# A routed expert kernel: conditional tiles moved in front of the last four static ones, and a skipped fallback path rewritten as a loop

## The chip, the cores and the metric

One core of a Trainium2 chip. The metric is device time in microseconds (us) of one execution. A profile is one execution, and its span (first to last instruction) is some 1.7 us shorter than the time of the same execution. Ratios and their intervals use only executions that the records call fast, on the same chip; the medians of the experiments are of all executions, slow ones included.

## The reference

Two stages in fp32. The first is chunked attention (4 batches, 8 heads, 768 tokens, heads of 64). The second is a mixture of 8 experts: each token goes to one expert, by an argmax over its logits or by inheriting the expert of the token in front of it.

```python
for s in range(S):
    fresh_e = int(np.argmax(logits[b, s]))
    e = fresh_e if s == 0 or local_gate[b, s] < 0.5 else prev_e
    prev_e = e
    p = softmax(logits[b, s])
    h = np.maximum(x[b, s] @ w1[e], 0.0)          # 512 -> 1024
    out[b, s] = p[e] * (h @ w2[e])                # 1024 -> 512
```

## The kernel before

Attention makes x, a router finds the expert of each token, and GpSimd scatters the rows to a DRAM buffer sorted by expert. The experts then work on tiles of 128 rows of one expert: gather the rows (GpSimd), turn (transpose) them on TensorE (`g_ps`, copied to SBUF by VectorE), first product (`h_ps`, relu by ScalarE), second product (`y_ps`, scaled by ScalarE), scatter to the output (GpSimd). 3072 tokens fill at least 24 tiles, which are static code. Up to 7 more are needed when experts' counts don't divide by 128; those are conditional on a count known only at run time, and with this input three of them run. The place behind them where all engines go on with unconditional code is called the join.

```python
for i in range(SURE):                            # SURE = 24
    ...                                          # (cut: gathers and weight loads ahead)
    w1_sb, w2_sb = tile_w[i]
    ht = hidden(xt, w1_sb, between.get(i, {}))   # 64 matmul instructions, relu
    ...
    if i + 1 < SURE:                             # the next tile's rows, turned ahead
        ahead = rows_turned(tiles, at_i, tile_xs[i + 1])
    stored = product(ht, w2_sb, tile_xs[i], past)   # 16 matmul instructions, scale, scatter
    xt, past = ahead

n_tiles = nc.values_load(n_i, ...)
for i in range(SURE - EARLY, NTILE - EARLY):     # the conditional tiles, at the end
    ctx.enter_context(tc.If(n_tiles > i))
    here = rest[:, i + EARLY - SURE]
    w1_sb, w2_sb = weights(late, i, pools[(i + EARLY) % 3])
    xt, past = rows_turned(late, i, here)        # turned when its turn comes
    product(hidden(xt, w1_sb), w2_sb, here, past)
```

The fast path takes exponentials without subtracting the maximum. It counts sums that stay in range, and if one doesn't, a general path computes everything again. Before, that path was the same function, unrolled a second time. With this input it is skipped; the branch that jumps over it is called the kept branch, after the count that it tests.

```python
everything(tc, *args, kept_i)
kept = nc.values_load(kept_i, ...)
with tc.If(kept < NT * H):
    everything(tc, *args, None)                  # the whole kernel once more, with shifted scores
```

## Time and profile before

| | before |
|---|---|
| time, median of 3 runs | 529.16 us |
| profiled span | 527.6 us |
| TensorE busy | 503.5 us (95%) |
| tile 0's first h starts at | 112.08 us |
| TensorE's last matmul ends at | 509.56 us |
| from there to the end | 18.02 us |

The last two rows come from the timeline of TensorE: the start of the last group, 502.52, plus its length, 7.03, with the nanoseconds that the view rounds off. Everything that argues about the end of the program below uses this one figure: span minus end of the last matmul. The profile calls TensorE PE, VectorE DVE, ScalarE ACT, GpSimd POOL and SyncE SP. In the page, the digits in 40 slices are busy tenths. In a view by source line, each row is operation, count, shortest/median/longest in ns, first and last start in us; a "q" behind an engine marks an instruction of its sequencer alone, which no busy figure counts.

### The profile page before, as it was taken

How to read it: one execution, taken by the hardware profiler on the slowest of the kernel's cores; microseconds unless marked ns; L12 is line 12 of the kernel's file. 1: busy time of each engine (PE TensorE's matmuls, PEld its weight loads, DVE VectorE, ACT ScalarE, POOL GpSimd, SP SyncE). 2: the span in 40 equal slices, each digit the busy share in tenths (PEclk: the TensorE clock that was granted, in tenths of full speed). 3: DMA queues.
4: the chain of work that ended last, by engine and by line, in shares of the span. 5: the costliest groups of instructions: out<-in, count | busy, mean ns of one | idle time of the engine just before them, and what ended most of it. 6: DMA issues, size and time to landing. Idle time of an engine off the chain costs nothing. (4 is left out here: it accounts for less than half of the span.)

```text
span 527.6 us, 9418 instructions
## 1 busy us (share of the span) xinstructions
PE 503.5 (95%) x3602; PEld 384.3 (73%) x3602; DVE 97.2 (18%) x361; ACT 113.0 (21%) x234; POOL 97.6 (19%) x142
## 2 busy tenths in 40 slices
PE   8999999999999999999999999999999999999960
PEld 5998989887677777777777777777777777777630
DVE  1456767653330000000000000000000000000000
ACT  3556555521101111111110111110110110111000
POOL 3000233444332111111001111122211011000000
PEclk9999999999999999999999999999999999999995
DMA  9987796799999999999889888899999899860000
GB/s 300 369 251 231 228 331 207 217 399 382 409 344 410 409 409 410 408 353 350 321 314 332 330 320 325 312 325 339 343 359 349 327 338 335 303 237 22 22 7 3
DMA packets 52761, 158.00 MB, mean 299 GB/s; under 512 B 7707, under 2 KB 11805, under 8 KB 52704
## 3 DMA queue, kind: packets, MB, share of 16 engines
q1 hardware_dynamic: 44352, 135.40, 71.0%
q0 software_dynamic: 6720, 20.78, 10.3%
q10 hardware_dynamic: 1632, 1.08, 0.7%
q8 instruction: 33, 0.54, 0.4%
q14 instruction: 24, 0.20, 0.1%
HBM read 144.62 MB, written 13.40 MB: 300 GB/s over the span
## 5 line engine op out<-in xcount | busy, mean ns | idle before, releaser
L647 PEld LDWEIGHTS h_ps<-gxt,w_sb 128*128 128x128 f32 x1664 | 189.6, 192 | 13.6 <-issue 10.5
L647 PE MATMUL h_ps<-gxt,w_sb 128*128 128x128 f32 x1664 | 190.6, 275 | 2.4 <-DVE gxt L583 1.6
L658 PE MATMUL y_ps<-w_sb,ht 128*128 128x512 f32 x416 | 182.8, 592 | 0.0
L658 PEld LDWEIGHTS y_ps<-w_sb,ht 128*128 128x128 f32 x416 | 77.0, 190 | 87.0 <-issue 85.9
L583 DVE COPY gxt<-g_ps 128x512 f32<-128x512 f32 x27 | 18.7, 692 | 315.9 <-PE g_ps L581 315.7
L650 ACT ACTIVATE ht<-h_ps 128x512 f32<-128x512 f32 x54 | 32.2, 597 | 156.4 <-PE h_ps L647 155.0
L663 POOL DMA_INDIRECT out_dram<-y,to x27 | 27.3, 1011 | 201.1 <-ACT y L662 166.6
L662 ACT ACTIVATE y<-y_ps,xs 128x512 f32<-128x512 f32 x24 | 16.5, 687 | 162.1 <-PE y_ps L658 155.9
L519 PE MATMUL o_ps<-vt,pt 128*96 128x65 f32 x512 | 49.3, 249 | 0.3 <-PE l_ps L519 0.2
L519 PEld LDWEIGHTS o_ps<-vt,pt 128*96 128x96 f32 x512 | 46.1, 165 | 2.7 <-issue 0.6
L364 POOL DMA_INDIRECT x_dram<-x,row x32 | 30.8, 961 | 75.3 <-DVE pick L309 65.5
L519 PEld LDWEIGHTS s_ps<-qt,kt 64*128 64x128 f32 x512 | 29.9, 188 | 6.1 <-issue 2.7
L519 PE MATMUL s_ps<-qt,kt 64*128 64x96 f32 x512 | 32.7, 277 | 0.4 <-ACT pt L211 0.4
L211 ACT ACTIVATE pt<-s_ps,mask_mid 128x256 f32<-128x256 f32 x72 | 28.1, 482 | 6.8 <-PE s_ps L519 6.6
L221 DVE TENSOR_TENSOR x<-o_ps,rinvs 96x256 f32<-96x256 f32 x64 | 26.3, 418 | 1.5 <-DVE rinvs L220 0.3
L262 ACT COPY xt<-xt_ps 128x384 f32<-128x384 f32 x32 | 15.3, 479 | 33.9 <-PE xt_ps L519 33.9
L660 POOL TENSOR_TENSOR to<-xs,past_late 128x1 int32<-128x1 int32 x19 | 3.5, 185 | 98.6 <-DMA out_dram<-y,to 94.1
L475 POOL DMA_INDIRECT xs<-x_dram,rows_late x19 | 18.4, 966 | 12.5 <-DMA x_dram<-x,row 7.0
L220 DVE RECIPROCAL rinvs<-o_ps 96x4 f32<-96x4 f32 x64 | 10.5, 171 | 35.7 <-PE o_ps L519 34.0
L519 PE MATMUL xt_ps<-ident,x 96*128 96x96 f32 x128 | 16.0, 247 | 0.0
L581 PE MATMUL g_ps<-ident,xs 128*128 128x128 f32 x88 | 13.3, 274 | 0.0
L519 PEld LDWEIGHTS xt_ps<-ident,x 96*128 96x128 f32 x128 | 12.7, 148 | 0.0
(160 smaller groups left out, 178.8 us busy)
## 6 DMA issues: line engine op xcount, KB each, us to landing
w_sb<-in_w_dram SPq DMA_DIRECT2D x216, 512.0 KB, 7.4
kt<-in_k_dram SPq DMA_DIRECT2D x32, 256.0 KB, 4.3
vt<-in_v_dram SPq DMA_DIRECT2D x28, 260.0 KB, 4.5
qt<-in_q_dram SPq DMA_DIRECT2D x32, 192.0 KB, 4.2
vt<-in_v_dram ACTq DMA_DIRECT2D x4, 260.0 KB, 4.8
x_dram<-x,row POOLq DMA_INDIRECT x32, 7.0
out_dram<-y,to POOLq DMA_INDIRECT x27, 7.6
xs<-x_dram,rows_late POOLq DMA_INDIRECT x19, 7.0
```

The source lines that it names most:

```text
L211: nc.scalar.activation(pt[:, :, :, c], st[:, :, :, c], ACT.Exp, bias=m[:, g:g + 1], scale=SCALE)
L221: nc.vector.tensor_tensor(x[:, 0:D].rearrange("p (a u d) -> p u a d", u=2, d=DH)[:, u], o_ps[:, :, 0:DH], rinv.to_broadcast([QB, HP, DH]), ...
L262: nc.scalar.copy(xt, xt_ps)
L364: ins = nc.gpsimd.indirect_dma_start(out=x_dram[:, :], out_offset=bass.IndirectOffsetOnAxis(ap=row[:, n:n + 1], axis=0), in_=x[0:QB, n].bi ...
L475: ins = nc.gpsimd.indirect_dma_start(out=xs.bitcast(I32), out_offset=None, in_=x_dram[:, :], in_offset=bass.IndirectOffsetOnAxis(ap=rows[: ...
L519: return f if shifted else lambda *a, **k: tc.keep_in_program_order(f(*a, **k))
L583: nc.vector.tensor_copy(xt, g_ps)
L647: nc.tensor.matmul(h_ps[:, m], lhsT=w1_sb[:, kk, P * (g + m):P * (g + m) + P], rhs=xt[:, kk], start=(kk == 0), stop=(kk == DK - 1))
L650: nc.scalar.activation(ht[:, g:g + 4], h_ps, ACT.Relu)
L658: nc.tensor.matmul(y_ps, lhsT=ht[:, m], rhs=w2_sb[:, m], start=(m == 0), stop=(m == FK - 1))
L662: nc.scalar.activation(y, y_ps, ACT.Copy, scale=xs[:, D:D + 1])
L663: return nc.gpsimd.indirect_dma_start(out=out, out_offset=bass.IndirectOffsetOnAxis(ap=to, axis=0), in_=y, in_offset=None, bounds_check=NT ...
```

## The change

Four things. The conditional tiles stand in front of static tile 20, so that the program ends in static code, and each turns the next one's rows ahead. The general path is a compact one: attention in order, then a loop over experts whose results are masked, with plain DMAs only. Tile 0's rows are turned before the last transposes of x. The ranks are transposed one block earlier. The rest (shared constants, where the count of sums is taken, buffers) makes room for it.

```diff
+BRANCH = SURE - 4
 with tc.If(kept < NT * H):
-    everything(tc, *args, None)
+    general(tc, q, k, v, w_gate, w_local, w1, w2, out, ident, back)
```
```diff
+def general(...):
+    ...                                    # (cut: attention, logits, prob[token, expert] masked by the choice)
+    with tc.For_i(0, E, 1) as e:
+        one_e = bass.ds(e, 1)
+        for kk in range(DK):
+            nc.sync.dma_start(w1_sb[:, kk], w1[one_e, kk].rearrange("o p f -> p (o f)"))
+        ...
+        for n in range(NB):
+            ...                            # hidden and product of 96 rows, as above
+            nc.vector.scalar_tensor_tensor(y[:, n], y_ps, mine[:, n], y[:, n], ALU.mult, ALU.add)
+    nc.sync.dma_start(out.rearrange("(n p) d -> p n d", p=QB), y)
```
```diff
+def maybe_tiles(ctx, xts):
+    n_tiles = nc.values_load(n_i, ...)
+    for j in range(NTILE - SURE):
+        i = SURE - EARLY + j
+        ctx.enter_context(tc.If(n_tiles > i))
+        w1_sb, w2_sb = weights(late, i, wa)
+        ht = hidden(xts[j % 2], w1_sb)
+        if j + 1 < NTILE - SURE:
+            rows_turned(late, i + 1, rest[:, j + 1], xt=xts[(j + 1) % 2])
+        product(ht, w2_sb, rest[:, j], late[2][:, i:i + 1])
 for i in range(SURE):
+    if i == BRANCH:
+        maybe_tiles(held_xt[1:])
...
+    if i + 1 == BRANCH:
+        rows_turned(late, SURE - EARLY, rest[:, 0], xt=held_xt[1])
-(the conditional tiles behind the loop)
```
```diff
-            plan_at(after, n + 5, rows, b)
+            plan_at(after, n + 4, rows, b)
...
-    plan_at(after, NB - 1, first_turned)          # behind the transposes of x
+        if n == NB - 1:
+            first_turned()                        # in front of them
```

## The prediction

> **What bounds the kernel now.** I read the page first: TensorE is busy nearly everywhere, so the time is TensorE's own work plus its gaps plus what lies before and behind it.
>
> ```profile
> PE 503.5 (95%) x3602; PEld 384.3 (73%) x3602; DVE 97.2 (18%) x361; ACT 113.0 (21%) x234; POOL 97.6 (19%) x142
> PE   8999999999999999999999999999999999999960
> DMA  9987796799999999999889888899999899860000
> ```
>
> The reader is to see a wall of nines on PE, a last slice of 13.2 us with none of it, and DMA that falls silent four slices earlier. The chain of waits is no help here: it holds one scatter and 0.2% of the span. So I went to the timeline of PE around the place where the static tiles end and the conditional ones begin (start, length, group, and in brackets the idle time before it and its releaser).
>
> ```profile
> 441.57 0.60 PE L581 MATMUL g_ps<-ident,xs 128*128 128x128 f32 x4
> 442.01 7.03 PE L658 MATMUL y_ps<-w_sb,ht 128*128 128x512 f32 x16
> 448.88 7.31 PE L647 MATMUL h_ps<-gxt,w_sb 128*128 128x128 f32 x64
> 456.02 7.03 PE L658 MATMUL y_ps<-w_sb,ht 128*128 128x512 f32 x16
> 462.89 0.60 PE L581 MATMUL g_ps<-ident,x 128*128 128x128 f32 x4
> 464.28 7.41 PE L647 MATMUL h_ps<-gxt,w_sb 128*128 128x128 f32 x64 [0.78 <-DVE gxt L583]
> 471.52 7.03 PE L658 MATMUL y_ps<-w_sb,ht 128*128 128x512 f32 x16
> ```
>
> A static tile is h (64 matmuls), g (four transposes of the next tile's rows) and y (16 matmuls). From the starts in the same view: h to g 7.14 us, g to y 0.44, y to the next h 6.87, so 14.45 us a tile. The last static tile has no g and takes 14.01. A conditional tile turns its own rows first, and then waits 0.78 us for VectorE's copy: h starts at 464.28 and the next at 479.78, so 15.50 us. With this input three of the seven conditional tiles run (27 scatters of results, 24 static), the last ending on PE at 509.56. The span ends at 527.6: 18.0 us follow PE's last matmul. What is in them the views by source line show, of the branch over the general path (L89) and of the end of the program (L751); columns are operation, count, shortest/median/longest ns, first and last start.
>
> ```profile
> L89 PEldq COMPARE_BRANCH  x1: 3387/3387/3387, 510.4 to 510.4; - x1
> L89 POOLq COMPARE_BRANCH  x1: 55/55/55, 513.9 to 513.9; - x1
> L89 POOLq EVENT_SEMAPHORE  x6: 17/30/43, 516.7 to 517.1; - x6
> L89 POOLq INC_SWDGE_SEM  x1: 1981/1981/1981, 517.2 to 517.2; - x1
> ...
> L751 POOLq DRAIN  x3: 40/107/7509, 519.2 to 527.3; - x3
> ```
>
> This is GpSimd's chain. The last result is issued at 511.1, then come a first INC_SWDGE_SEM at the join of the conditional tiles (2.03 us from 511.3, in the view of the helper's line), the branch at 513.9, its next instruction only at 516.7, a second INC_SWDGE_SEM of 1.98 us, and a DRAIN of 7.51 us from 519.2, after which 0.9 us of barrier end the program. All of it is on the path.
>
> **What the Trainium skill says.** "Runtime: NRT & Kernel Launch", section "Instruction fetch mechanics": a taken branch whose target is not in the two blocks at hand waits for a fetch. The trace agrees: branches within the tiles take PE 65 to 86 ns, the jump over the general path 3.39 us, and GpSimd resumes 2.7 us after its own. "DMA: Bandwidth & Descriptors", section "Anatomy of one DMA — SWDGE (gpsimd) path", puts one transfer at about 2.0 us plus its bytes over 436 GB/s. A full tile's 128 rows of 2 KB would then need about 2.6 us when nothing else moves (an estimate from that page). The page of this trace has a median of 7.6 us beside weight loads but 2.4 us for the last scatter, which is alone. No page tells how long the drain at the end is.
>
> **The change, part by part.**
>
> 1. *Conditional tiles in front of the last four static ones, with the rows turned ahead.* Inside a conditional tile the next rows are now turned before y, as in a static one. Before, from h of static tile 20 (405.53) to the end at 509.56, seven tiles took 104.03 us. As six tiles of 14.45 and a last one without g they take 6 x 14.45 + 14.01 = 100.71: 3.3 us less. Against it stand three costs. The third conditional tile also turns the rows of a fourth that doesn't run: 0.44 us in excess. In static tile 19 two sets of rows are turned back to back through a single PSUM buffer (g_ps): if nothing fills the gap, the second waits for VectorE's copy of the first, about the 0.78 us above; y is ready soon and may be put in front, so I take 0.4. And the join behind the conditional tiles stands in PE's way now. The trace shows what a join does: each engine waits for its own semaphore. PE passed it 0.05 us after its last matmul, with a branch of 0.2 us behind it; ScalarE passed it only after the last y, 0.83 us after that matmul. The first h of static tile 20 needs a PSUM buffer that ScalarE frees, counted beyond ScalarE's join, so I expect h to start about 1.0 us after the last y matmul instead of overlapping it by 0.16: 1.1 us. The long branch fetch (3.46 us on PE from 503.4) lies under the 16 y matmuls already queued and is free in both. Net: -3.3 + 0.4 + 0.4 + 1.1 = -1.4 us.
>
> 2. *Weights around the branch.* Tile 20's weights sit in the third buffer and are loaded ahead. Those of tile 21 can start only when PE is past its join. A tile's 4.2 MB at the 400 GB/s that the page shows in its best slices are 10.5 us, the first halves about 6 to 7; PE has 14.45 us of tile 20 meanwhile. The conditional tiles share two buffers instead of three, with a tile between release and use. Hidden: 0.
>
> 3. *End of the program.* The last tile is static, so the join, with its 2.03 us INC_SWDGE_SEM, is no longer behind the last scatter, but in the middle, where GpSimd has 14 us to spare. That takes about 2.0 us off the chain. The general path is now a loop without GpSimd's own DMAs, so GpSimd's jump over it may hit code at hand: up to 2.7 us more, of which waiting for the last full scatter to land (2.6 us) eats part; I take 1.0. The 7.51 us DRAIN I leave. Net -3.0.
>
> 4. *Tile 0's rows turned ahead.* At 110.0 to 112.1 PE does r_ps, g, waits, h:
>
> ```profile
> 109.58 0.50 PE L519 MATMUL xt_ps<-ident,x 96*128 96x96 f32 x4
> 110.01 0.54 PE L519 MATMUL r_ps<-ident,rank 8*96 8x8 f32 x8
> 110.64 0.66 PE L519 MATMUL g_ps<-ident,xs 128*128 128x128 f32 x4
> 112.08 2.05 PE L519 MATMUL h_ps<-gxt,w_sb 128*128 128x128 f32 x16 [0.78 <-DVE gxt L583]
> ```
>
> With g ahead of the xt transposes, their 0.43 us lie over the copy; the ranks' transposes move one block earlier, where VectorE finishes their input just then (its multiplications ran until 107.76, PE came by at 107.4), so a little is given back. Net -0.4.
>
> 5. *Kept count in tile 0 instead of tile 4, zero row from the warm-up tile, constants shared, general path rewritten.* Same matmuls, or off the path: PE's warm-up starts at 1.5 us and the first scores at 8.0, long after the masks are ready. The general path does not run with this input (all sums are in range). 0.
>
> Sum: -1.4 - 3.0 - 0.4 = -4.8, so 529.16 - 4.8 is about 524.4 us.
>
> **The rivals.** *A stall behind the join:* the weights of tile 21 come late, or PE must fetch instructions after the join, 3.4 us by the branch above. For it: nothing can be issued across the join, and all engines pass it in the same few microseconds. Against it: slack of several microseconds in the weights, and a fetch that the queue of y matmuls hid before. With it the gain of part 1 is lost and the time is near 528; a late load of some 7 us would make it 532. *The end stays as it is:* if the drain absorbs what is taken out in front of it (it waits for something that started with the last scatter, 15.6 us before it ends), only parts 1 and 4 remain: 527.4. *The end shrinks much more:* if the drain's 7.5 us are work left by the INC_SWDGE_SEM, and the skip path has none of it any more, the end falls from 18 us to some 6 to 8, and the time to 514 to 518. For it: the DRAIN follows the second INC directly, and the new general path uses no GpSimd DMA. Against it: two other GpSimd drains in the final barrier are short, which says only that something was pending. *TensorE's work itself* can't change: same matmuls, same clock.
>
> **Range and chances.** Parts 1 and 4 are worked out from repeated durations and may be off by 1.5 us together; the end is the wide part, from 0 to 5 us of gain as likely values. The range is 520.5 to 527.5. Faster by over 2% (below 518.8) needs the shrunken drain: 0.06. Slower by over 2% (over 539.7) needs a stall of 10 us, which I see nowhere: 0.02. Within 2%: 0.92.
>
> **What would show it.** Right: h of a conditional tile following y without the 0.78 us wait; one gap of about 1.1 us on PE at the first tile behind the join, released by ScalarE; two sets of g in tile 19; no INC_SWDGE_SEM between the last scatter and the kept branch; the same DRAIN of about 7.5 us; 15 us from PE's last matmul to the end. Wrong: weights as releaser of h or y, a gap of 3 us or more at the join, a longer or missing drain, or slower matmuls.

## More of the kernel before

One chip, on which e1 to e4, their repeats, e10 and e11 ran, granted TensorE 94 to 96% of its clock even in the fast executions, and the kernel before took 565 us there instead of 529. (Seven of the nine runs of the kernel before that e10, e11 and the repeats are compared with are from an earlier call on that chip.)

## The result, and the profile after

520.85 us (median of 4 fast runs, 520.23 to 521.97) against 529.15 of the kernel before. The ratio is 0.9839, with a 95% interval from 0.9815 to 0.9864. That is 8.3 us less: inside the range, at its lower end, and within 2%. The prediction had 4.8.

The page after: TensorE's busy time is the same within 0.1 us, its matmuls are four more (the rows of a conditional tile that doesn't run), the empty last slice has gone, and DMA shows a hole near the end and then two full slices. SyncE asks for the weights of static tile 21 only at 449.6 us, released by TensorE at the join.

```profile
PE 503.4 (97%) x3606; PEld 384.5 (74%) x3606; DVE 98.0 (19%) x362; ACT 113.2 (22%) x234; POOL 96.8 (19%) x141
PE   8999999999999999999999999999999999999991
DMA  9987797599999999999898899999998881299200
```

Where the 8.7 us of the span went, by marks that both timelines have:

| stretch | before | after | change | predicted |
|---|---|---|---|---|
| start to tile 0's first h | 112.08 | 111.95 | -0.13 | -0.4 |
| to the end of the last matmul | 397.47 | 396.05 | -1.43 | -1.4 |
| to the end of the program | 18.02 | 10.88 | -7.14 | -3.0 |

**The tiles.** The timeline of TensorE in the changed kernel around static tile 19 (start, length, group; idle time and releaser in brackets):

```profile
398.09 0.60 PE L677 MATMUL g_ps<-ident,xs 128*128 128x128 f32 x4
398.53 1.02 PE L754 MATMUL y_ps<-w_sb,ht 128*128 128x512 f32 x2
399.48 0.66 PE L677 MATMUL g_ps<-ident,x 128*128 128x128 f32 x4
399.97 6.17 PE L754 MATMUL y_ps<-w_sb,ht 128*128 128x512 f32 x14
405.98 0.60 PE L677 MATMUL g_ps<-ident,x 128*128 128x128 f32 x4
```

Two sets of rows are turned in tile 19, and two matmuls of y stand between them while VectorE copies the first: no wait. The third g belongs to the first conditional tile, which turns the rows of the second at once. Around the join:

```profile
434.88 0.60 PE L677 MATMUL g_ps<-ident,x 128*128 128x128 f32 x4
435.32 7.31 PE L743 MATMUL h_ps<-held_xt,w_sb 128*128 128x128 f32 x64
442.47 7.03 PE L754 MATMUL y_ps<-w_sb,ht 128*128 128x512 f32 x16
450.37 7.41 PE L743 MATMUL h_ps<-held_xt,w_sb 128*128 128x128 f32 x64 [0.87 <-ACTq _compat.py:109]
```

The waits of 0.78 us in front of each conditional h are gone. One gap of 0.87 us is left behind the join, and its releaser is ScalarE's sequencer at its own join. The instruction INC_SWDGE_SEM of GpSimd's queue, which stood behind the last scatter, is at the join here too:

```profile
_compat.py:109 POOLq INC_SWDGE_SEM  x1: 1939/1939/1939, 451.2 to 451.2; - x1
```

**The end.** GpSimd's part in the views of the branch over the general path, and of the end of the program:

```profile
L92 POOLq COMPARE_BRANCH  x1: 55/55/55, 509.7 to 509.7; - x1
```
```profile
L856 POOLq DRAIN  x3: 40/113/7862, 510.2 to 518.6; - x3
```

Before, 5.3 us lay between this branch and the drain (513.9 to 519.2), with a late start (GpSimd's next instruction came only at 516.7) and a second INC_SWDGE_SEM. Now it is 0.5 us, and there is no INC_SWDGE_SEM behind the last scatter at all. The drain itself is 7.86 us long, against 7.51.

**The start.** The last three microseconds in front of tile 0:

```profile
107.41 0.50 PE L613 MATMUL xt_ps<-ident,x 96*128 96x96 f32 x4
107.83 0.64 PE L613 MATMUL r_ps<-ident,rank 8*96 8x8 f32 x8
108.47 0.64 PE L613 MATMUL l_ps<-ident,lt_sb 128*96 128x128 f32 x4
108.95 1.50 PE L613 MATMUL o_ps<-vt,pt 128*96 128x65 f32 x16
110.28 0.61 PE L613 MATMUL g_ps<-ident,xs 128*128 128x128 f32 x4
110.73 0.49 PE L613 MATMUL xt_ps<-ident,x 96*128 96x96 f32 x4
111.95 2.05 PE L613 MATMUL h_ps<-held_xt,w_sb 128*128 128x128 f32 x16 [0.73 <-DVE held_xt L680]
```

g is ahead of xt as planned, and yet h still waits 0.73 us for VectorE's copy: g ends at 110.89, but VectorE is at work on x until about 111.3 and copies g only from 111.23 to 111.90. Whether the start gained anything is taken up under e5.

### The profile page after: what moved, and what is told of

It reads as the page before. It is cut to its first block, busy times and chain, and to the rows that moved or that the text cites. A ratio compares the mean times of both kernels' runs of the same rounds, so it can differ in the third digit from the quotient of the medians.

```text
span 518.9 us, 9415 instructions
## 1 busy us (share of the span) xinstructions
PE 503.4 (97%) x3606; PEld 384.5 (74%) x3606; DVE 98.0 (19%) x362; ACT 113.2 (22%) x234; POOL 96.8 (19%) x141
## 5 line engine op out<-in xcount | busy, mean ns | idle before, releaser
L743 PEld LDWEIGHTS h_ps<-gxt,w_sb 128*128 128x128 f32 x1408 | 160.7, 192 | 10.1 <-issue 10.0
L743 PE MATMUL h_ps<-gxt,w_sb 128*128 128x128 f32 x1408 | 161.1, 275 | 0.0
L680 DVE COPY gxt<-g_ps 128x512 f32<-128x512 f32 x22 | 15.2, 691 | 273.5 <-PE g_ps L677 273.4
L743 PE MATMUL h_ps<-held_xt,w_sb 128*128 128x128 f32 x256 | 29.3, 275 | 0.9 <-ACTq _compat.py:109 0.9
L743 PEld LDWEIGHTS h_ps<-held_xt,w_sb 128*128 128x128 f32 x256 | 28.9, 192 | 1.7 <-ACTq _compat.py:109 1.7
```

What stands on the lines that cost most here:

```text
L680: nc.vector.tensor_copy(xt, g_ps)
L743: nc.tensor.matmul(h_ps[:, m], lhsT=w1_sb[:, kk, P * (g + m):P * (g + m) + P], rhs=xt[:, kk], start=(kk == 0), stop=(kk == DK - 1))
```

## The experiments

Two questions: which parts of the end shrank and why (the prediction had 3.0 of the 7.1 us), and what the drain is that remains. My theory after the result: three separate terms left GpSimd's chain. They are the join's INC_SWDGE_SEM, a fetch of code behind the kept branch, and a second INC_SWDGE_SEM that exists only because the skipped path contained GpSimd DMAs. The rivals: the move alone, or the general path alone, did it all.

### e1 and e2: one half of the change each

e1 is the kernel before with `maybe_tiles` in front of tile 20 (two buffers were merged to make room), and nothing else. e2 is the changed kernel with the conditional tiles put back behind the loop.

```diff
 # e1: the kernel before
+        if i == BRANCH:
+            maybe_tiles(held_xt[::-1])
 ...
     with tc.If(kept < NT * H):
         everything(tc, *args, None)      # unchanged
```
```diff
 # e2: the kernel after
-        if i == BRANCH:
-            maybe_tiles(held_xt[1:])
 ...
+    for i in range(SURE - EARLY, NTILE - EARLY):
+        ctx.enter_context(tc.If(n_tiles > i))
+        ...                              # as in the kernel before
```

> The kernel before with the conditional tiles moved in front of the last four static ones and their rows turned ahead, but with the old general path (a second unrolled copy of everything) and the old start. Theory: the end of the program shrank for two separate reasons, and this run has only the first: no join, with its INC_SWDGE_SEM, behind the last scatter. PE's last matmul at about 508.1 us (1.4 earlier than before), then about 15.4 us to the end instead of 18.0: one INC_SWDGE_SEM of 2 us and a wait of 2.7 us behind the branch over the general path are still there; time near 525. Rival A (the move alone does it all): 10.9 us to the end as in the changed kernel, time near 520.9. Rival B (the move does nothing to the end): 18 us, time near 527.7.

> The changed kernel with the conditional tiles put back behind the last static one, turning their own rows, but with the new general path. Theory: this run has only the second reason: the branch over the general path finds its target at hand (2.3 us less) and no counts of GpSimd DMAs are made up for behind it (2.5 us less), while the join of the conditional tiles keeps its INC_SWDGE_SEM: PE's last matmul at about 509.4, then 13 to 13.5 us to the end; the conditional tiles again show waits of 0.78 us; time near 524.3. Rival A of the first run would have 18 us to the end, time near 529; the opposite rival (the general path alone does it all) 10.9 us, time near 522.

Both results were correct. The times, 562.6 and 564.5 us against 564.8 of the kernel before, are from the chip with the low clock. The intervals of their ratios (0.993 to 1.014, and 0.988 to 1.013) can't resolve 4 us. The end of the program shows no dependence on TensorE's clock (e8 and e11 below, with granted clocks of 0.999 and 0.948, both end in 5.95 us): 15.23 us in e1, 13.23 in e2, where the theory had 15.4 and 13 to 13.5, and no rival fits. GpSimd in e1, branch over the old path:

```profile
L90 POOLq EVENT_SEMAPHORE  x6: 17/30/43, 543.2 to 543.7; - x6
L90 POOLq COMPARE_BRANCH  x1: 55/55/55, 540.6 to 540.6; - x1
L90 POOLq INC_SWDGE_SEM  x1: 1986/1986/1986, 543.8 to 543.8; - x1
```

2.6 us from the branch to the next instruction and 1.99 us of INC_SWDGE_SEM are both still there. e2 shows the opposite half:

```profile
_compat.py:109 POOLq INC_SWDGE_SEM  x1: 2021/2021/2021, 552.8 to 552.8; - x1
```

The join's INC is back behind the last scatter, and the kept branch has none. So the move took 2.8 us off the end (18.02 to 15.23) and the new general path 4.8 us (18.02 to 13.23).

I ran both once more for their times, unchanged, and drew the same chip:

> e1_front_old_general again, unchanged, because that chip ran at a granted clock of 0.95 and its times told nothing. Theory: time near 524.8 (1.4 from the tiles, 2.8 from the end), 15.2 us behind PE's last matmul. Rival A 520.9, rival B 527.7.

> e2_end_new_general again, unchanged, for the same reason. Theory: time near 524.2 (4.8 from the end, little else), 13.2 us behind PE's last matmul. Rivals 529 and 522.

560.9 and 560.9 us, ratios 0.9975 (0.986 to 1.009) and 0.998 (0.987 to 1.009): inconclusive again as times. The ends repeat, 15.27 and 13.23 us.

### e3 and e4: the two terms of the general path, each by itself

Both edits are in code that is never executed.

```diff
 # e3
-    nc.sync.dma_start(out.rearrange("(n p) d -> p n d", p=QB), y)
+    nc.gpsimd.dma_start(out.rearrange("(n p) d -> p n d", p=QB), y)
```
```diff
 # e4
+    pad = one.tile([P, 4], F32, name="pad")
+    for _ in range(600):
+        nc.gpsimd.memset(pad, 0.0)
```

> The changed kernel with one edit in the general path, which is not executed: its final store is issued by GpSimd instead of SP. Theory: a path that would have issued a GpSimd DMA makes the path around it make up for its count: an INC_SWDGE_SEM of about 2 us returns behind the kept branch, and it first waits for the last scatter to land (4.4 us after PE's last matmul): the drain starts 2.6 to 4.3 us later, time 523.5 to 525.2. Rival (the INC came from the size or form of the old path, not from its DMAs): unchanged, 520.9.

> The changed kernel with 600 small GpSimd memsets added to the general path, which is not executed. Theory: GpSimd's jump over the path now leaves the code at hand and has to fetch: about 2.3 us between the kept branch and the next GpSimd instruction, no INC_SWDGE_SEM, drain 2.3 us later, time near 523.2. Rival (GpSimd resumed late before because it waited for something, not for code): unchanged, 520.9.

Both correct, both on the low clock (561.3 and 560.3 us, intervals 0.987 to 1.008 and 0.984 to 1.009, so again nothing from the times). The ends: 12.52 us in e3 and 12.95 us in e4, against 10.88. In e3 an INC_SWDGE_SEM stands behind the kept branch again:

```profile
L92 POOLq COMPARE_BRANCH  x1: 55/55/55, 551.6 to 551.6; - x1
L92 POOLq INC_SWDGE_SEM  x1: 1960/1960/1960, 552.1 to 552.1; - x1
```

In e4 there is none, but the next instruction comes 2.9 us behind the branch instead of 0.5:

```profile
L92 POOLq COMPARE_BRANCH  x1: 55/55/55, 546.4 to 546.4; - x1
L92 POOLq EVENT_SEMAPHORE  x1: 17/17/17, 549.3 to 549.3; - x1
```

Both terms are shown. e3 was a partial miss: I expected GpSimd to wait for the last scatter to land before its INC and hence 2.6 to 4.3 us. It did not (the INC starts 2.18 us behind the last matmul), and the end grew by 1.64. In both runs the drain is 7.51 us again, not 7.86. In the changed kernel it starts 0.34 us before the last scatter's own instruction ends (2.17 and 2.51 us behind the last matmul), and 7.5 us count from there. That accounts for most of why the two halves of the change, 2.8 and 4.8, give 7.1 and not 7.6 together.

### e5: the start of tile 0

```diff
-            plan_at(after, n + 4, rows, b)
+            plan_at(after, n + 5, rows, b)
```

> The changed kernel with the transposes of the ranks (r_ps) put back one block later, as before; tile 0's rows stay ahead of the last transposes of x. Theory: the move of r_ps cost what turning ahead gained: where r_ps stands between xt_ps and l_ps, l_ps waits for ScalarE's copy to free one of two PSUM buffers, and PE takes 3.30 us from that xt_ps to the next s_ps instead of 3.00, twice, and about 0.4 at the last move, where r_ps waits for VectorE. Without it (full clock) those stretches are 3.00 again, the wait of tile 0's first h for the copy falls from 0.73 to under 0.3, and that h starts about 1 us earlier; time about 1 us less than the changed kernel. Rival (the start of tile 0 is set by VectorE's work or the gather in front of it): no change, the wait only moves.

Correct, 520.3 us against 529.0 (ratio 0.9826, 0.9806 to 0.9846): beside the changed kernel's 0.9839 no difference. Part of the theory holds. Where r_ps no longer stands between xt_ps and l_ps, TensorE takes 3.01 us again from that xt_ps to the next s_ps (56.62 to 59.63), where the changed kernel takes 3.30. The changed kernel, then e5:

```profile
52.88 2.03 PE L613 MATMUL s_ps<-qt,kt 64*128 64x96 f32 x32
56.25 0.50 PE L613 MATMUL xt_ps<-ident,x 96*128 96x96 f32 x4
56.68 0.54 PE L613 MATMUL r_ps<-ident,rank 8*96 8x8 f32 x8
57.32 0.64 PE L613 MATMUL l_ps<-ident,lt_sb 128*96 128x128 f32 x4
59.55 2.03 PE L613 MATMUL s_ps<-qt,kt 64*128 64x96 f32 x32
```
```profile
53.26 2.03 PE L613 MATMUL s_ps<-qt,kt 64*128 64x96 f32 x32
56.62 0.50 PE L613 MATMUL xt_ps<-ident,x 96*128 96x96 f32 x4
56.96 0.60 PE L613 MATMUL l_ps<-ident,lt_sb 128*96 128x128 f32 x4
59.16 0.54 PE L613 MATMUL r_ps<-ident,rank 8*96 8x8 f32 x8
59.63 2.03 PE L613 MATMUL s_ps<-qt,kt 64*128 64x96 f32 x32
```

But at the last block the rival is right:

```profile
109.99 0.63 PE L613 MATMUL g_ps<-ident,xs 128*128 128x128 f32 x4 [0.16 <-DMA xs<-x_dram,rows_early]
110.46 0.50 PE L613 MATMUL xt_ps<-ident,x 96*128 96x96 f32 x4
111.52 0.54 PE L613 MATMUL r_ps<-ident,rank 8*96 8x8 f32 x8 [0.57 <-ACT xt L362]
112.00 2.05 PE L613 MATMUL h_ps<-held_xt,w_sb 128*128 128x128 f32 x16
```

r_ps now needs one of the two PSUM buffers that g_ps and xt_ps hold, and waits 0.57 us. Tile 0's h starts at 112.00, nearly as in the changed kernel (111.95), but that time alone misleads: e5 came to the first s_ps shown 0.37 us later, by work in which the two sources don't differ. From that s_ps to h are 58.74 us in e5 and 59.07 in the changed kernel. So 0.34 us was gained, not the expected 1: of the 0.60 that the first two batches gave back, the last block lost 0.26 again.

### e6: who holds TensorE at the join

```diff
-            h_ps = hps.tile([P, 4, P], F32, name="h_ps")
+            h_ps = (ps or hps).tile([P, 4, P], F32, name="h_ps", tag="xps" if ps else "h_ps")
 ...
-        ht = hidden(xt, w1_sb, between.get(i, {}))
+        ht = hidden(xt, w1_sb, between.get(i, {}), xps if i == BRANCH else None)
```

> The changed kernel with one edit: the h of static tile 20, the first behind the join, is made in the two PSUM buffers of the attention stage, which no conditional tile uses. Theory: PE stood 0.87 us at the join because the h buffers are counted as free only when ScalarE is past its join, after the last y. With other buffers PE waits for its own join alone: the gap falls to 0.35 to 0.5 us. Rival (PE's own branch and refill make the gap): still 0.87.

Correct, 520.3 us against 529.0 (ratio 0.9839, 0.9822 to 0.9855). The time doesn't resolve 0.4 us. The timeline does:

```profile
453.24 4.29 PE L743 MATMUL h_ps<-held_xt,w_sb 128*128 128x128 f32 x36 [0.44 <-PEq _compat.py:109]
```

0.44 us, released by TensorE's own sequencer. So of the 0.87 us, half was ScalarE's join and half is TensorE's own. From tile 0's h to the last matmul are 395.62 us here and 396.05 in the changed kernel.

### e7 and e8: what the drain is

e7 gives wrong results (the last tile goes to the first 128 rows), to take GpSimd off the end.

```diff
 # e7
+        if plain:                            # the last tile only
+            return nc.sync.dma_start(out[0:P], y).ins
         return nc.gpsimd.indirect_dma_start(
```
```diff
 # e8
         stored = product(ht, w2_sb, tile_xs[i], past)
+        if i == SURE - 2:
+            with tc.issue_after(stored):
+                nc.gpsimd.drain()
```

> The changed kernel with wrong results on purpose: the last tile is stored to the first 128 rows by a plain DMA of SP, in place of GpSimd's scatter. It measures what the drain behind the last scatter costs. Theory: the drain lasts 7.5 us from the later of its start and GpSimd's last work, so it now runs beside the last tile, and the end takes what y, the store and the final barrier need: about 5 us behind PE's last matmul instead of 10.9; 6 us less than the changed kernel. Rival (the drain waits for the end of something else, or starts only after all stores): 10 to 11 us to the end.

> The changed kernel with one more GpSimd drain, directly behind the scatter of the last tile but one. It tells whether the drain at the end is work that piled up over the run or a fixed cost. If it piled up: the first drain is as long as the last one was or longer, and the last one falls well under 7.5 us, with the end under 10 us behind PE's last matmul. If fixed (my theory): both last 7.5 us and the end stays at 10.9.

e7 (wrong): 515.9 us, ratio 0.9749 (0.9733 to 0.9765), end 6.38 us. The drain ran beside the last tile, from 496.0 to 503.8:

```profile
L858 POOLq DRAIN  x3: 40/113/7777, 496.0 to 513.9; - x3
```

So in the changed kernel the drain costs about 4.5 us of the end (10.88 against 6.38, with a plain store in place of the scatter).

e8 proved my theory wrong. The result is correct, and the drain at the end shrank. The additional drain, and the ones at the end:

```profile
L819 POOLq DRAIN  x1: 8628/8628/8628, 495.6 to 495.6; - x1
```
```profile
L859 POOLq DRAIN  x3: 46/112/2262, 510.5 to 514.0; - x3
```

8.63 us are spent beside TensorE's last tile, and 2.26 us are left for the end, which is now 5.95 us long. SyncE is its limit now: it sees the last scatter's semaphore 4.43 us behind the last matmul, just when the drain ends (4.46), and GpSimd goes on at 5.15, after SyncE's last instructions. The time was 515.95 us in one run, against 529.01 of the kernel before and 520.3 of e5 and e6 on the same chip.

### e10: does the drain work off what piled up?

The same line behind the scatter of tile 10 (`if i == 10`), with 32 of the 91 GpSimd DMAs still to come.

> The changed kernel with the additional GpSimd drain behind the scatter of tile 10, with some 33 GpSimd DMAs still to come. Theory A (a drain works off what piled up since the last one, in proportion): with 1.9 us for one DMA and 7.5 for about 91, the last drain takes about 4 us after the last scatter, the end comes about 7.3 us behind PE's last matmul. Theory B (the first drain after GpSimd DMAs pays once, later ones don't): 2.3 us and an end at 5.9 as in e8_drain_before. Theory C (only a drain close before the end helps): 7.5 and 10.9.

Correct, 554.1 us on the low clock. The drain at the end:

```profile
L859 POOLq DRAIN  x3: 46/113/3792, 547.7 to 552.1; - x3
```

3.79 us, with an end of 6.81: A's 4 and 7.3, not B's 2.3 and 5.9 nor C's 7.5 and 10.9. From the end of the last scatter's instruction the drain takes 7.52 us with 91 DMAs since the program's start, 3.45 with 32 since the earlier drain and 1.93 with one. So at the end of the program it is shorter the less lies between it and the drain before. What counts (DMAs, descriptors, elapsed time) is open, since all fall together, and so is whether the shortest one waited for the scatter's landing, which came at the same moment. The early drain of this run doesn't fit a proportion:

```profile
L819 POOLq DRAIN  x1: 9485/9485/9485, 314.4 to 314.4; - x1
```

From the end of its scatter's instruction it takes 8.24 us with 59 DMAs behind it; e8's early one, counted alike, takes 7.43 with 90. I didn't separate what it waited for among the weight loads. The join of this run shows one more thing:

```profile
_compat.py:109 POOLq INC_SWDGE_SEM  x1: 758/758/758, 488.8 to 488.8; - x1
```

0.76 us, where the same instruction takes 1.94 to 2.03 in every other run. This is the only run with a drain in front of the join, so an earlier drain seems to shorten the INC too; one run, not tested further.

### e11: what the runs point to, together

```diff
+        if i == SURE - 2:
+            with tc.issue_after(stored):
+                nc.gpsimd.drain()
-            plan_at(after, n + 4, rows, b)
+            plan_at(after, n + 4 if b > 1 else n + 5, rows, b)
 (and the edit of e6)
```

> What the runs so far point to, with right results: the changed kernel, a GpSimd drain behind the scatter of the last tile but one, own PSUM buffers for the first h behind the join, and the transposes of the ranks one block later for the first two batches only. From e8_drain_before 4.9 us, from e6_own_banks 0.4, from the ranks 0.6 (two stretches of 3.30 us back at 3.00): about 6 us less than the changed kernel, near 515, faster than before by over 2.5%.

Correct, 553.5 us (6 runs) on the chip with the low clock, where the kernel before took 564.8: ratio 0.9857, 0.978 to 0.993, which leaves open whether it is faster by over 2%. Its end is 5.95 us and the gap at the join 0.51 us at a granted clock of 0.948. The expected 515 at full clock is not confirmed. e8 is the fastest correct version that was timed on an undisturbed chip. It was timed once; that it beats both kernels rests on its end, which the profile shows.

| run | last matmul to the end, us | what GpSimd does there |
|---|---|---|
| before | 18.02 | INC at the join, late start, INC, drain 7.51 |
| e1, e1b | 15.23, 15.27 | late start, INC, drain 7.51 |
| e2, e2b | 13.23, 13.23 | INC at the join, drain 7.58 |
| after, e5, e6 | 10.88 | drain 7.86 |
| e3 | 12.52 | INC, drain 7.51 |
| e4 | 12.95 | late start, drain 7.51 |
| e7 (wrong results) | 6.38 | nothing: drained beside the last tile |
| e10 | 6.81 | drain 3.79 |
| e8, e11 | 5.95 | drain 2.26, 2.27 |

## Why the prediction was right or wrong

**Part 1, the tiles: right in sum, and nearly so by term.** Net -1.4 predicted, -1.43 measured. The three conditional tiles save 3 x (15.50 - 14.45) = 3.15 us, predicted 3.3: the sum of 100.71 counts the last y as the 6.87 us to a next start, where the 104.03 counts its 7.03 to the end. The join cost 1.14 us, predicted 1.1, with the releaser it named: from y at 442.47 to h at 450.37 are 7.90 us, against 6.87 from one y to the next h elsewhere, and from that h to the next g 7.25 against 7.14. The double turning cost 0.14 us beyond the extra transposes, predicted 0.4; the rows of the fourth tile, 0.44, as predicted. That the sum fits to 0.03 us is luck: the slip of 0.16 and the 0.26 too many for the double turning nearly cancel.

**Part 2, the weights: right.** No wait for a load shows at h or y behind the join; the weights of tile 21, asked for from 449.6 us, had landed by 463.6, before its h at 464.93. One argument for the rival of a stall was misread: the engines do not pass the join in the same few microseconds. In the kernel before, SyncE passed it at 472.5 us, VectorE at 495.3, and the other three from 509.6 to 511.3.

**Part 3, the end: right in direction, with one term missing and two too small.** Net -3.0 predicted, -7.14 measured, outside the 0 to 5 us that the prediction called likely for the end; the total stayed in the range with 0.35 us to spare. The term "2.0 us off the chain" for the join's INC measured 2.8 (e1): with the INC, what stands around it goes too (from the last scatter's start to the kept branch 2.80 us before, 0.16 in e1). The term "up to 2.7 us more ... I take 1.0" for code at hand should have been about 2: e4 shows 2.07 for it. The wait for the landing that was to eat part of it did not come: the drain starts 2.17 us behind the last matmul, the scatter lands at 4.33. What failed is that the second INC_SWDGE_SEM was not on the list of what goes. The prediction saw that "the general path is now a loop without GpSimd's own DMAs" and drew only the fetch from it. It named the missing INC in a rival, tied it there to a vanishing drain, and gave that 6%. e3 shows that one GpSimd DMA in the skipped path brings an INC of 1.96 us back, 1.64 us at the end. (The three terms, 2.8, 2.07 and 1.64, make 6.5 of the 7.14; the overlap of 0.34 us shown under e4 takes part of the last two, and the rest was not split.) "The 7.51 us DRAIN I leave" was right for this change (7.86), and so was not to follow the rival of a drain that absorbs all: without an earlier drain, it counts from the end of GpSimd's last work and not from a fixed point.

**Part 4, tile 0: wrong; the edits cost a little.** -0.4 predicted, -0.13 measured at tile 0's h, but that is no effect of the edits. In four profiles of kernels with this same start (after, e6, e7, e8) this h starts between 111.78 and 112.24 us, because the s_ps group in front of the first edited block already starts between 52.70 and 53.16 (53.17 before). Counted from that group, h comes after 58.92 us in the kernel before (one profile) and after 59.07 to 59.08 in the four: 0.16 later. The failed step is "a little is given back". Each of the first two moves of r_ps cost 0.30 us (3.00 us from xt_ps to the next s_ps before, 3.30 after), because r_ps between xt_ps and l_ps makes l_ps need the PSUM buffer that xt_ps still holds, one of two: l_ps at 57.32 is released by ScalarE's copy of xt. The last block, with g ahead, gained 0.44 (4.99 us from its xt_ps to h before, 4.55 after). The prediction looked at VectorE's finish for the last batch only, and not at the buffers. e5 shows that putting all of them back doesn't help in the last block: two buffers are too few for g, xt and r in a row.

**Part 5: right.** The count in tile 0 and the rest show nothing on the path.

## What to carry to other kernels

Read the end of a program from the last matmul on, in the sequencers' own instructions, which no busy figure counts: here 18 us stood there, more than all gaps of TensorE together. Code that is never run can cost time at the branch around it (here 1.64 us for a GpSimd DMA in it and 2.07 us for a longer jump, e3 and e4), so keep a rare path free of the engine that ends last, and end the program in straight code. If a drain stands at the end, try an earlier one of the same engine in its idle time: here one added drain took 4.9 us more off the end (e8, e11), and the results stayed correct. To judge an edit, count from a mark just in front of it: the start of this program alone varied by 0.5 us between profiles.

## What the Trainium skill lacked or had wrong

- *VectorE: DVE Perf Modes*, section "The DRAIN you can't avoid", says of the drains that the runtime puts at a program's ends that they are about 12 ns, constant, on all five engines. The drains here are listed under the program's own closing line, so the page may not mean them. The other engines' fit it (7 to 17 ns), GpSimd's does not: 7.51 us in the kernel before, 7.86 in the changed one, 3.79 and 2.26 with an earlier drain. No page has a figure for it.
- No page has that this drain shrinks when an earlier one has run: 8.63 us beside the last tile, then 2.26 at the end (e8).
- No page has INC_SWDGE_SEM: 1.94 to 2.03 us each, at every join around skipped GpSimd DMAs (the conditional tiles' in all other runs, the kept branch in before, e1 and e3), and 0.76 us at the one join behind an earlier drain (e10).
- *Advanced Engine Details and Errata*, section "Control Flow Timing", gives about 108 ns for a compare-and-branch. Here most take 34 to 86 ns. In the kernel before, TensorE's jump over the general path takes 3.39 us; GpSimd's takes 55 ns, but its next instruction comes only 2.7 us later.
- *Runtime: NRT & Kernel Launch*, section "Instruction fetch mechanics", agrees with e4 on the stall behind a taken branch whose target is far, but gives no duration: 2.4 us more on GpSimd than where the skipped code is short (2.9 against 0.5).
